# Loading a weight matrix in pairs of pieces to all partitions, with a re-ordered opening, in a retention and feed-forward kernel

## The chip, the cores and the metric

The kernel runs on one NeuronCore of a Trainium2 chip. TensorE (PE) multiplies matrices and writes PSUM; VectorE (DVE), ScalarE (ACT) and GpSimd (POOL) do element-wise work; SyncE (SP) issues most transfers between DRAM and SBUF, which the core's 16 DMA engines carry out. The engines run their own instruction streams in order and wait for one another through semaphores. The metric is the device time of one execution in microseconds (us), the median of several runs; less is better.

## The reference

q, k and v are [8 batches, 8 heads, 576 positions, 64] in float32. Each head is a retention layer: scores are q k^T / 8, multiplied by a decay gamma^(s - t) where s >= t and by 0 elsewhere, with gamma = 1 - 2^(-5 - head), and then multiplied by v. The result is laid out as x, [4608 tokens, 512 channels], channel = head x 64 + d. Then a feed-forward network: h = max(x w_in, 0), out = (h * h) w_out, with w_in [512, 2048] and w_out [2048, 512]. The two weights come as float64, as numpy makes them; the output is float32.

```python
scores = scale * np.matmul(q, k.transpose(0, 1, 3, 2))
ret = scores * Dmat[None, :, :, :]
attn_out = np.matmul(ret, v)
x = attn_out.transpose(0, 2, 1, 3).reshape(B * S, H * D)
h = np.maximum(x @ w_in, 0.0)
out = h * h @ w_out
```

## The kernel before

**Chunks.** The retention part goes over 40 chunks of up to 128 positions (five to a batch: four of 128, one of 64). For a chunk `load(i)` issues three transfers, for q, k and v, each as [positions, heads, 64]; `scale_q` and `scale_v` multiply q and v by powers of gamma (mostly on GpSimd); `turn(i)` transposes q and k on TensorE (L430) into a PSUM tile `t_ps` of two banks, and ScalarE (L434) and VectorE (L435) copy one bank each into the SBUF tile `qk`; `scores(i)` makes q k^T per half chunk of 64 positions (L461), and VectorE masks it (L471, from chunk 4 on L473). `retain_a`, `retain_b` and `retain_c` multiply with v (L559), add the contribution of the running state (L508) and let the state grow (L553); ScalarE copies the state (L487) and the finished piece of x (L536) to SBUF. From chunk 11 on a chunk is turned in another way (`flip`, L404 and L419).

**Weights.** w_in is used as 16 pieces of [512, 128], `pieces[0..15]`. A piece is fetched by `fetch_w` (L206) as raw 64-bit words into one of six places, and turned into float32 by `round_parts`: `one` (L220) takes the exponents, `two` (L224) the upper fraction bits, `beside` (L228, L229, ScalarE) makes the scale and the lower fraction, `three`, `four` and `five` (L232, L235, L238) put the number together. `convert(n)` issues the next n of these parts; `N_ALONE` says from which piece on the first two parts of a piece are put ahead of the last three of the one before. In SBUF a piece has partition p = 64 b + d, b = 0 or 1, d = 0..63, and column block c = 0..3, for row 256 b + 64 c + d of w_in. Before the change one piece is two transfers, one for each b, to 64 partitions each.

**The feed-forward part.** Tokens go in 9 blocks of 512. For block 0 `first_in(j)` multiplies all or half of its x with piece j (L664: four matmuls, 512 or 256 columns), takes max(.., 0) (L669) and squares it (L672). From block 1 on the products follow a Strassen-like scheme of seven products for eight (`ffn_in`, L700; the groups h_a, h_b, h_c), and the second matrix product (L1042) follows after all chunks are done. Squared values go to DRAM (`g_dram`) and come back for the second product.

**What sets the order.** The order of every engine's instructions is written out in the program: the calls from L845 to L901 for chunks 0 to 4, then a loop over the chunks (L902) in which `ffn(i, half)` interleaves feed-forward steps, with a table of points (`PACE`) for how many. Engines take their instructions in exactly that order, also SP its transfers, so a transfer that must wait for a buffer holds all behind it. For the first block the loop does three `step`s per chunk, a `convert(6)` beside each (L791 to L796); the second halves of the pieces whose first half was done in the opening (`N_HALF` = 3) are steps too. `fetch_raw(n)` fetches the next n pieces if a place is free; after the opening each finished piece calls it.

**Unread products.** `warm` (L824) issues matmuls on a constant tile whose result nobody reads. There are two forms: 128x128 on the whole array, and pairs on quarters of it, 64 rows by 512 columns.

Of the kernel before, what the change touches and what calls it, by code (L numbers as in the profile page):

```python
# [9 lines left out]
F32 = mybir.dt.float32  # L10
# [30 lines left out]
def kernel(  # L41
# [62 lines left out]
    work3 = first.enter_context(tc.tile_pool(name="work3", bufs=3))  # L104
    work2 = first.enter_context(tc.tile_pool(name="work2", bufs=2))
    ps_x = first.enter_context(tc.tile_pool(name="ps_x", bufs=1, space=PS))
    ps_t = first.enter_context(tc.tile_pool(name="ps_t", bufs=1, space=PS))
    ps_u = first.enter_context(tc.tile_pool(name="ps_u", bufs=1, space=PS))

# [20 lines left out]
    def load(i, names="qkv"):  # L132
# [4 lines left out]
        for name, pool, src in (("q", ld3, q), ("k", ld5, k), ("v", ld4, v)):  # L137
            if name not in names:
# [7 lines left out]

    pieces = [(0, m, e) for m in range(N_M) for e in range(2)]
    pieces += [(1, mq + mh * N_MQ, e) for mq in range(N_MQ) for mh in range(2) for e in range(2)]  # L150
    N_W1 = N_DF
    N_ALONE = 4
    N_HALF = 3
    stage = [W[5].rearrange("p (o s f) -> p o s f", o=4, s=NP),
             W[6][:, 0:3 * NP * 128].rearrange("p (o s f) -> p o s f", o=3, s=NP)]
    N_RAW = 6
    raw_all = [W[4 + j // 3][:, (j % 3) * 1024:(j % 3 + 1) * 1024] for j in range(N_RAW)]
    exp_all = [W[4 + j][:, 3072:3584] for j in range(3)]
    wide = moe_w_in.dtype != F32

    def raw_of(j):
        return raw_all[j % N_RAW] if j < N_W1 else raw_all[(j - N_W1) % 3]

    def exp_of(j):
        return exp_all[j % 2] if j < N_W1 else exp_all[2 * (j % 2)]

    def rows(half, n=64):
        return slice(64 * half, 64 * half + n)

    def piece_src(j):  # L170
        wi, m, e = pieces[j]
        f = (m + e * N_M) * 128
        return moe_w_out[f:f + 128, :].rearrange("p (c f) -> p c f", c=N_DM)

    def in_parts(j):

        wi, m, e = pieces[j]
        f = (m + e * N_M) * 128  # L180
        for half in range(2):
            of = slice(half * d_model // 2, (half + 1) * d_model // 2)
            yield rows(half), moe_w_in[of, f:f + 128].rearrange("(c p) f -> p c f", p=D)

    def piece_dst(j):
        wi, m, e = pieces[j]
# [5 lines left out]
    def as_dst(j, t):  # L192

        if pieces[j][0] == 0:
            return t.rearrange("p (c f) -> p c f", c=N_DM)
        return t.rearrange("p (o s f) -> p o s f", o=2, s=2)

    def fetch_w(j):
        if j >= len(pieces) or not wide:
            return  # L200
        to = raw_of(j).bitcast(I64)
        if pieces[j][0]:
            nc.sync.dma_start(to.rearrange("p (c f) -> p c f", c=N_DM), piece_src(j))
        else:
            for at, part in in_parts(j):
                nc.sync.dma_start(to[at].rearrange("p (c f) -> p c f", c=N_DM), part)  # L206

    def round_parts(j):
        words = raw_of(j).bitcast(U32).rearrange("p (n two) -> p n two", two=2)
        lo, hi = words[:, :, 0], words[:, :, 1]
        frac = raw_of(j).rearrange("p (n two) -> p n two", two=2)[:, :, 0]
        exp = exp_of(j).bitcast(U32)
        t = piece_dst(j)
        bits = t.bitcast(U32)

        def one():
            nc.vector.tensor_scalar(exp, hi, 20, 0x7FF, op0=ALU.logical_shift_right, op1=ALU.bitwise_and)  # L220

        def two():

            nc.vector.tensor_scalar(bits, as_dst(j, hi), 0xFFFFF, 0x100000, op0=ALU.bitwise_and, op1=ALU.bitwise_or)  # L224

        def beside():

            nc.scalar.activation(exp, exp, AF.Relu, bias=exp_bias[:, 0:1], scale=2.0 ** 23)  # L228
            nc.scalar.activation(frac, lo, AF.Copy, scale=2.0 ** -52)  # L229

        def three():
            nc.vector.scalar_tensor_tensor(t, bits, 2.0 ** -20, as_dst(j, frac), op0=ALU.mult, op1=ALU.add)  # L232

        def four():
            nc.vector.tensor_tensor(t, t, as_dst(j, exp_of(j)), op=ALU.mult)  # L235

        def five():
            nc.vector.scalar_tensor_tensor(bits, as_dst(j, hi), 0x80000000, bits, op0=ALU.bitwise_and, op1=ALU.bitwise_or)  # L238

        if not wide:  # L240
            if pieces[j][0]:
                return [lambda: nc.sync.dma_start(t.rearrange("p o s f -> p (o s) f"), piece_src(j))] + [lambda: None] * 5
            return [lambda: [nc.sync.dma_start(t[at], part)
                             for at, part in in_parts(j)]] + [lambda: None] * 5
        return [one, two, beside, three, four, five]

    def sum_w_in(mp):
# [51 lines left out]
    def fetch_raw(count):  # L299

        for _ in range(count):
            if n_raw[0] < min(N_W1, n_made[0] + N_RAW):
                fetch_w(n_raw[0])
                n_raw[0] += 1


    def w_in_parts():
# [34 lines left out]
    fetch_raw(1)  # L342
    load(1, "v")
    load(2)
    fetch_raw(2)

    make_identity(nc, ident)

# [31 lines left out]
    def scale_q(i, engine):  # L380
        ci, cs = chunks[i][1], chunks[i][3]
        t = loaded[i][0][:cs]
        engine.tensor_tensor(t, t, dv[:cs, :, NCH + ci:NCH + ci + 1].to_broadcast([cs, H, D]), op=ALU.mult)  # L383
# [2 lines left out]


    N_TURN = 11
    N_ONE = N_TURN - 1
    moves = []  # L390

    def new_qk(i):
        t = work3.tile([128, 2, HP, C], F32, tag="qk", name="qk")
        st[i]["qT"], st[i]["kT"] = t[:, 0, :, :], t[:, 1, :, :]
        return t
# [23 lines left out]
            nc.scalar.copy(*moves.pop(0)[2:])  # L419
            count -= 1  # L420

    def turn(i):

        cs = chunks[i][3]
        n_h = cs // CH
        p = ps_t.tile([128, 2, 512], F32, tag="t", name="t_ps").rearrange("p h (j d t) -> p h j d t", j=2, d=HP)
        for j in (1, 0):
            for hp in range(HP):
                for h in range(n_h):
                    nc.tensor.transpose(p[:, h, j, hp, :], loaded[i][j][rows(h), 2 * hp:2 * hp + 2, :],  # L430
                                        ident[rows(h), rows(h)])
        to = new_qk(i)[:, :, :, :cs].rearrange("p j d (h t) -> p j d h t", h=n_h)
        if n_h == 2:
            nc.scalar.copy(to[:, :, :, 0, :], p[:, 0, :, :, :])  # L434
            nc.vector.tensor_copy(to[:, :, :, 1, :], p[:, 1, :, :, :])  # L435
        else:
            nc.scalar.copy(to[:, 1].rearrange("p d h t -> p h d t"), p[:, :n_h, 1, :, :])
            nc.vector.tensor_copy(to[:, 0].rearrange("p d h t -> p h d t"), p[:, :n_h, 0, :, :])

    def scores(i, part=False):  # L440

        b_, ci, c0, cs = chunks[i]
        if i < N_EARLY:

            sc = [ps_f.tile([128, 512], F32, tag="f", name="sc_ps")[:, 0:256].rearrange("p (h t) -> p h t", h=HP) for e in range(2)]
        else:
            both = ps_t.tile([128, 2, 512], F32, tag="t", name="sc_ps")[:, :, 0:256].rearrange("p e (h t) -> p e h t", h=HP)
            sc = [both[:, e, :, :] for e in range(2)]
        st[i]["sc"] = sc
        st[i]["both"] = None if i < N_EARLY else both  # L450
        if part:
            return
        for hp in range(HP):
            score(i, hp)
        masked(i)
# [365 lines left out]
        held[0] = busy[0] = False  # L821


    def warm(count, wide):  # L824
        t = ps_f.tile([128, 512], F32, tag="f", name="idle_ps")
        for _ in range(count):
            if wide:
                nc.tensor.matmul(t[:, 0:128], lhsT=idle, rhs=idle, start=True, stop=True)
            else:
                for b in range(2):  # L830
                    nc.tensor.matmul(t[rows(b), :], lhsT=idle[rows(0), rows(b)], rhs=idle[rows(0), 0:1].to_broadcast([64, 512]),
                                     start=True, stop=True, skip_group_check=True)

    def loads(i):
        if i < N_TURN - 1:
# [6 lines left out]
        if i + 3 < N_CH:  # L842
            load(i + 3, "v")

    warm(6, True)  # L845
    scale_q(0, nc.vector)
    turn(0)
    load(3)
    scores(0)
    scale_q(1, nc.gpsimd)  # L850
    warm(1, False)
    turn(1)
    fetch_raw(1)
    retain_a(0)
    convert(3)
    scores(1)
    scale_q(2, nc.gpsimd)
    retain_b(0)
# [1 line left out]
    load(4)  # L860
    fetch_raw(2)
    convert(2)
    retain_a(1)
    turn(2)
    convert(1)
    retain_b(1)
    retain_c(1)
    load(5)
    fetch_raw(1)
    convert(3)  # L870
    first_in(0, (0,))
    convert(1)
    scores(2)
    scale_q(3, nc.gpsimd)
    retain_a(2)
    convert(2)
    turn(3)
    first_in(1, (0,))
    convert(3)
    retain_b(2)  # L880
    retain_c(2)
    load(6)
    fetch_raw(1)
    convert(1)
    scores(3)
    convert(2)
    scale_q(4, nc.gpsimd)
    first_in(2, (0,))
    convert(3)
    retain_a(3)  # L890
    turn(4)
    retain_b(3)
    retain_c(3)
    load(7)
    fetch_raw(2)
    step()
    scores(4)
    convert(3)
    scale_q(5, nc.gpsimd)
    step()  # L900
    convert(5)  # L901
    for i in range(N_EARLY + 1, N_CH + 1):  # L902
        if i > N_ONE:
            move(C, i)
# [287 lines left out]
```

## Time and profile before

| | |
|---|---|
| three runs | 967.30, 967.76, 970.39 us; median 967.76 |
| the profiled execution | 970.93 us, its span on the core 969.2 us |
| granted TensorE clock, mean | 0.989 |
| TensorE busy | 949.6 us, 98% of the span |
| VectorE busy | 783.1 us, 81% |
| ScalarE busy | 337.3 us, 35% |
| GpSimd busy | 133.3 us, 14% |
| chain that ended last | TensorE 92%, VectorE 4%, transfers 2% |
| first products of block 0 (L664), in all | 61.7 us, 152 rows |

The profile comes from one execution. A row of a group gives the source line, the engine, the operation, the tile written and the tiles read, the shape, the count, and the busy time with the mean of one. A window row gives for a stretch the busy time and count of each engine, then the granted TensorE clock (1.00 is full), the mean busy share of the 16 DMA engines (packets can overlap, so it can pass 1) and what they moved. A wait row gives who waited, for whom, how long in total, how often, and the longest. The chain of waits follows the work that ended last back to the start, step by step. The slices cut the span into 40 equal parts of 24.2 us; a digit is a tenth of busy share.

### The profile page before, as it was taken

The page shows a single profiled execution, that of the slowest core. Times are in us where ns is not written, and L with a number is a line of the kernel's source. Part 1 is how long each engine was busy: PE and PEld are TensorE (multiplying, and loading weights), DVE is VectorE, ACT ScalarE, POOL GpSimd, SP SyncE. Part 2 cuts the span into 40 slices and gives each one's busy share as a digit, 9 for nine tenths or more (in the row PEclk, how much of TensorE's full clock was granted, in tenths as well). Part 3 has the DMA queues.
Part 4 walks back from the last instruction along what each step waited for, and adds up shares of the span by engine and source line. Part 5 has one row for each costly group of instructions (what it writes and reads, how often), then busy time and mean ns, then how long its engine had stood idle before and what let it go on. Part 6 is the DMA issues. An engine that isn't in the chain of part 4 may idle for free.

```text
span 969.2 us, 23541 instructions
## 1 busy us (share of the span) xinstructions
PE 949.6 (98%) x10000; PEld 852.4 (88%) x10000; DVE 783.1 (81%) x1447; ACT 337.3 (35%) x808; POOL 133.3 (14%) x121
## 2 busy tenths in 40 slices
PE   7799999999999999999999999999999999999998
PEld 6645688888888888888888899999999999999998
DVE  3599799988889887987976597887888787787876
ACT  3345375765765767657621000000000000000000
POOL 2221233123133123122110000000000000000000
PEclk7999999999999999999999999999999999999999
DMA  9996667676857867776168966445354454524251
GB/s 197 202 226 165 153 167 211 179 226 208 208 151 220 242 166 203 199 213 170 61 253 330 366 238 244 165 158 185 115 202 155 159 195 170 203 99 174 88 175 44
DMA packets 169705, 181.39 MB, mean 187 GB/s; under 512 B 115840, under 2 KB 130176, under 8 KB 162944
## 3 DMA queue, kind: packets, MB, share of 16 engines
q1 hardware_dynamic: 167520, 179.37, 61.7%
q8 instruction: 78, 1.28, 0.6%
q10 hardware_dynamic: 2080, 0.52, 0.3%
q14 instruction: 27, 0.22, 0.1%
HBM read 109.36 MB, written 70.52 MB: 186 GB/s over the span
## 4 chain that ended last, share of the span: by engine, by line
PE 92%; DVE 4%; DMA 2%; issue 1%; ACT 1%; SPq 0%; DVEq 0%
PE o_b L1042 17%; PE h_b L700 16%; PE o_a L1042 11%; PE o_c L1042 11%; PE h_a L700 11%; PE h_c L700 10%; PE h_ps L664 6%; PE x_ps L559 3%; PE sc_ps L461 2%; PE u_ps L553 1%; DMA g<-g_dram 1%; PE x_ps L596 1%; PE t_ps L430 1%; PE x_ps L508 1%; DMA q_ld<-in_q_dram 0%
## 5 line engine op out<-in xcount | busy, mean ns | idle before, releaser
L700 PE MATMUL h_b<-room,w 128*128 128x256 f32 x768 | 183.6, 382 | 2.8 <-DVE room L719 1.8
L419 ACT COPY qk<-flip 32x256 f32<-32x256 f32 x416 | 167.3, 402 | 6.2
L700 PEld LDWEIGHTS h_b<-room,w 128*128 128x128 f32 x768 | 144.3, 190 | 24.3 <-DVE room L719 2.6
L1042 PE MATMUL o_b<-w,room 128*128 128x128 f32 x1168 | 144.4, 275 | 0.2 <-DVE room L994 0.2
L1042 PEld LDWEIGHTS o_b<-w,room 128*128 128x128 f32 x1168 | 137.2, 192 | 0.4 <-DVE room L994 0.4
L1042 PE MATMUL o_c<-w,room 128*128 128x128 f32 x1008 | 123.0, 275 | 0.0
L700 PE MATMUL h_a<-room,w 128*128 128x256 f32 x512 | 122.0, 381 | 0.0
L700 PE MATMUL h_c<-room,w 128*128 128x256 f32 x512 | 121.7, 380 | 0.0
L1042 PEld LDWEIGHTS o_c<-w,room 128*128 128x128 f32 x1008 | 117.7, 192 | 0.0
L1056 ACT COPY r<-o_a 128x128 f32<-128x128 f32 x53 | 14.2, 267 | 272.8 <-PE o_a L1042 236.9
L700 PEld LDWEIGHTS h_a<-room,w 128*128 128x128 f32 x512 | 96.5, 190 | 13.8 <-issue 0.5
L700 PEld LDWEIGHTS h_c<-room,w 128*128 128x128 f32 x512 | 96.7, 190 | 13.3
L1042 PE MATMUL o_a<-w,a 128*128 128x128 f32 x688 | 85.7, 275 | 0.0
L717 POOL TENSOR_TENSOR room<-room 128x512 f32<-128x512 f32 x32 | 36.1, 1129 | 337.5 <-ACT room L716 326.2
L1042 PEld LDWEIGHTS o_a<-w,a 128*128 128x128 f32 x688 | 81.2, 192 | 0.1
L707 DVE SCALAR_TENSOR_TENSOR room<-room 128x512 f32<-128x512 f32 x96 | 70.0, 730 | 3.3
L664 PE MATMUL h_ps<-room,w 128*128 128x512 f32 (+1 forms) x152 | 61.7, 555 | 3.6 <-DVE w L238 2.3
L559 PEld LDWEIGHTS x_ps<-qk,v_ld 64*64 64x64 f32 x1152 | 45.7, 140 | 15.7 <-issue 13.8
L559 PE MATMUL x_ps<-qk,v_ld 64*64 64x64 f32 x1152 | 56.7, 229 | 1.7 <-DVE qk L471 1.0
L383 POOL TENSOR_TENSOR q_ld<-q_ld,dv 128x512 f32<-128x512 f32 (+1 forms) x39 | 45.6, 1170 | 78.9 <-DMA q_ld<-in_q_dram 72.6
L480 POOL TENSOR_TENSOR v_ld<-v_ld,dv 128x512 f32<-128x512 f32 (+1 forms) x40 | 52.7, 1318 | 16.9 <-DMA v_ld<-in_v_dram 16.9
L664 PEld LDWEIGHTS h_ps<-room,w 128*128 128x128 f32 x152 | 28.7, 197 | 27.7 <-issue 23.6
(107 smaller groups left out, 1350.9 us busy)
## 6 DMA issues: line engine op xcount, KB each, us to landing
g_dram<-room SPq DMA_DIRECT2D x32, 1280.0 KB, 5.7
a<-g_dram SPq DMA_DIRECT2D x30, 1024.0 KB, 5.8
room<-g_dram SPq DMA_DIRECT2D x15, 1024.0 KB, 6.1
w<-w_dram SPq DMA_DIRECT2D x7, 1792.0 KB, 9.9
out_dram<-room SPq DMA_DIRECT2D x17, 512.0 KB, 3.3
q_ld<-in_q_dram SPq DMA_DIRECT2D x32, 256.0 KB, 6.3
w<-in_moe_w_in_dram SPq DMA_DIRECT2D x32, 256.0 KB, 5.8
w<-in_moe_w_out_dram SPq DMA_DIRECT2D x16, 512.0 KB, 4.2
```

Source lines behind the costliest of these rows:

```text
L383: engine.tensor_tensor(t, t, dv[:cs, :, NCH + ci:NCH + ci + 1].to_broadcast([cs, H, D]), op=ALU.mult)
L419: nc.scalar.copy(*moves.pop(0)[2:])
L430: nc.tensor.transpose(p[:, h, j, hp, :], loaded[i][j][rows(h), 2 * hp:2 * hp + 2, :], ident[rows(h), rows(h)])
L461: nc.tensor.matmul(st[i]["sc"][e][rows(h), hp, :], lhsT=st[i]["kT"][rows(e), hp, t], rhs=st[i]["qT"][rows(e), hp, t], start=True, stop=Tru ...
L480: nc.gpsimd.tensor_tensor(vs[:cs], vs[:cs], dv[:cs, :, ci:ci + 1].to_broadcast([cs, H, D]), op=ALU.mult)
L559: return [lambda hp=hp, e=e, b=b: nc.tensor.matmul(x_at(hp, e, b, h), lhsT=s["vs"][rows(h), 2 * hp + e, :], rhs=s["ret"][rows(h), e, hp, : ...
L664: nc.tensor.matmul(p.rearrange("p h t -> p (h t)"), lhsT=w[:, c, :], rhs=xT[0][:, c, lo * HT:hi * HT], start=(c == 0), stop=(c == N_DM - 1))
L700: nc.tensor.matmul(p[:, mm, :], lhsT=w[:, c, :], rhs=xs[n][right][:, c, :], start=(j in OPENS and mm == 0 and c == 0), stop=(j in CLOSES a ...
L707: nc.vector.scalar_tensor_tensor(t, t, 0.0, t, op0=ALU.max, op1=ALU.mult)
L717: nc.gpsimd.tensor_tensor(g["A11"], g["A11"], g["A11"], op=ALU.mult)
L1042: nc.tensor.matmul(p, lhsT=s["lefts"][left][:, m, :], rhs=w_out[j][:, m, WO_SLOT[right], :], start=(i in OPENS and m == 0), stop=(i in CLO ...
L1056: nc.scalar.copy(r[:, 0, 0:128], p)
```

## The change

The change has four parts. (1) w_in is fetched by `fetch_in` to all 128 partitions in four transfers, one for each column block c: pieces 0 and 1 alone, the others two pieces at a time, 256 columns together, into one of three places for pairs. The order of the pieces changes so that two neighbours in w_in's columns follow one another. The parts of `round_parts` read the raw words through patterns with one more dimension. (2) Chunks 0 to 3 are turned into two PSUM tiles of one bank each (`ps_e`) instead of one tile of two; `turn` is split in `turn_in` and `turn_out`, and chunk 2 has both of its copies on ScalarE. The pool is closed before chunk 4, and the one tile of two banks takes its place. (3) The unread products have one form, 128 rows by 256 columns on the whole array; there are 14 of them in seven places. (4) The calls of the opening stand in another order, with one half product less (`N_HALF` = 2) and one whole product more before the loop.

```diff
-    pieces = [(0, m, e) for m in range(N_M) for e in range(2)]
+    pieces = [(0, 2 * mp + mm, e) for mp in range(N_MP) for e in range(2) for mm in range(2)]
-    N_HALF = 3
+    N_HALF = 2
-    N_RAW = 6
-    raw_all = [W[4 + j // 3][:, (j % 3) * 1024:(j % 3 + 1) * 1024] for j in range(N_RAW)]
+    N_PAIR = 3
+    raw_one = [W[4 + j][:, 2048:3072] for j in range(2)]
+    raw_two = [W[4 + j][:, 0:2048] for j in range(N_PAIR)]
...
-    def in_parts(j):
-        wi, m, e = pieces[j]
-        f = (m + e * N_M) * 128
-        for half in range(2):
-            of = slice(half * d_model // 2, (half + 1) * d_model // 2)
-            yield rows(half), moe_w_in[of, f:f + 128].rearrange("(c p) f -> p c f", p=D)
+    def in_rows(c, j, count):
+        wi, m, e = pieces[j]
+        f = (m + e * N_M) * 128
+        return moe_w_in.rearrange("(b c d) f -> c b d f", b=2, d=D)[c][:, :, f:f + 128 * count]
...
-            for at, part in in_parts(j):
-                nc.sync.dma_start(to[at].rearrange("p (c f) -> p c f", c=N_DM), part)
+    def fetch_in(j, count):
+        to = (raw_one[j] if count == 1 else raw_two[(j // 2 - 1) % N_PAIR]).bitcast(I64).rearrange("p (c f) -> p c f", c=N_DM)
+        for c in range(N_DM):
+            nc.sync.dma_start(to[:, c, :], in_rows(c, j, count))
...
     def fetch_raw(count):
         for _ in range(count):
-            if n_raw[0] < min(N_W1, n_made[0] + N_RAW):
-                fetch_w(n_raw[0])
-                n_raw[0] += 1
+            j = n_raw[0]
+            if j < N_W1 and (j < 2 * N_PAIR + 2 or n_made[0] >= j - 2 * N_PAIR + 2):
+                count = 1 if j < 2 else 2
+                fetch_in(j, count)
+                n_raw[0] += count
...
-    def turn(i):
-        p = ps_t.tile([128, 2, 512], F32, tag="t", name="t_ps").rearrange("p h (j d t) -> p h j d t", j=2, d=HP)
+    def turn_in(i, js=(1, 0)):
+            if i < N_EARLY:
+                p = [ps_e.tile([128, 512], F32, tag=f"e{h}", name="t_ps") for h in range(2)]
+            else:
+                t = ps_t[0].tile([128, 2, 512], F32, tag="t", name="t_ps")
+                p = [t[:, h, :] for h in range(2)]
...
+    def turn_out(i, engines=(0, 1)):
+        copies = (nc.scalar.copy, nc.vector.tensor_copy)
+            for h in range(2):
+                copies[engines[h]](to[:, :, :, CH * h:CH * h + CH], p[h])
...
-    def warm(count, wide):
+    def warm(count):
+            nc.tensor.matmul(t[:, 0:256], lhsT=idle, rhs=idle[:, 0:1].to_broadcast([128, 256]), start=True, stop=True)
```

The opening, as it stands after the change:

```python
    warm(5)
    scale_q(0, nc.vector)
    turn_in(0, (1,))
    scale_q(1, nc.gpsimd)
    warm(3)
    turn_in(0, (0,))
    turn_out(0)
    load(3)
    warm(1)
    scores(0)
    turn(1)
    fetch_raw(1)
    retain_a(0)
    scores(1)
    scale_q(2, nc.gpsimd)
    retain_b(0)
    retain_c(0)
    load(4)
    fetch_raw(2)
    convert(2)
    warm(1)
    retain_a(1)
    convert(1)
    warm(1)
    retain_b(1)
    retain_c(1)
    load(5)
    convert(3)
    turn(2, (0, 0))
    warm(2)
    scores(2)
    scale_q(3, nc.gpsimd)
    convert(2)
    first_in(0, (0,))
    retain_a(2)
    convert(1)
    retain_b(2)
    retain_c(2)
    load(6)
    convert(3)
    first_in(1, (0,))
    turn(3)
    warm(1)
    scores(3)
    scale_q(4, nc.gpsimd)
    convert(3)
    retain_a(3)
    early.close()
    ps_t[0] = first.enter_context(tc.tile_pool(name="ps_t", bufs=1, space=PS))
    turn(4)
    convert(3)
    retain_b(3)
    retain_c(3)
    load(7)
    fetch_raw(1)
    step()
    step()
    scores(4)
    convert(6)
    scale_q(5, nc.gpsimd)
    step()
    convert(6)
```

## The prediction

> **What bounds the kernel now.** I read the page's slices first, then the ten-microsecond windows, then the chain of waits, then the transfers.
>
> ```profile
> PE   7799999999999999999999999999999999999998
> ...
> DVE  3599799988889887987976597887888787787876
> ...
> PEclk7999999999999999999999999999999999999999
> DMA  9996667676857867776168966445354454524251
> ```
>
> One slice is 24.2 us. TensorE is busy in all but the first two or three slices, so from about 50 us on whatever shifts TensorE's stream shifts the end one for one. The transfer engines are full in exactly the first three slices. The windows show the same opening (busy us of PE, PEld, DVE, ACT, POOL, then granted clock, transfer share, GB/s):
>
> ```profile
> 0.00:10.00 10.00, 5.64 (x62) 4.74 (x64) 1.65 (x4) 1.87 (x2) 3.42 (x12) 0.88 0.97 182
> 10.00:20.00 10.00, 9.14 (x202) 7.00 (x202) 5.04 (x9) 3.97 (x8) 3.18 (x3) 0.50 1.17 219
> ...
> 30.00:40.00 10.00, 6.63 (x147) 5.13 (x141) 4.52 (x10) 3.40 (x8) 2.86 (x3) 0.83 1.11 205
> ...
> 50.00:60.00 10.00, 9.53 (x64) 4.55 (x64) 9.83 (x17) 3.31 (x7) 3.04 (x2) 0.83 0.97 190
> ```
>
> and so do narrower windows, and the first 60 us in one:
>
> ```profile
> 53.00:58.00 5.00, 5.00 (x10) 2.14 (x9) 4.93 (x10) 1.01 (x2) 0.39 (x1) 0.76 1.08 224
> 63.50:65.00 1.50, 1.50 (x5) 0.47 (x3) 1.45 (x3) 0.64 (x2) 0.00 (x0) 1.00 1.05 346
> ...
> 0.00:60.00 60.00, 47.09 (x744) 34.26 (x744) 33.08 (x61) 20.76 (x41) 17.27 (x24) 0.83 1.07 198
> ```
>
> In the first 60 us TensorE idles 60 - 47.1 = 12.9 us and runs part of the rest at half clock (0.50 from 10 to 20 us). The last chain pieces of the first stage fix my mark, the end of the first block's last product:
>
> ```profile
> 107.15 3.63 PE h_ps L664 x8
> 110.78 1.73 PE h_a L700 x8
> ```
>
> The mark is 110.78 us. The same work stands ahead of it in both kernels, and from there the streams are alike: time after = time before + shift of the mark. The profiled execution took 970.93 us (span 969.2 us); the median of the three runs is 967.76 us, 3.2 us less, and I put the shift on the median.
>
> The waits that the change touches (engine, line, releaser: us in total, times, longest), and the transfers of w_in (32 of 256 KB, us from issue to landing):
>
> ```profile
> DVE qk L435 <- ACT qk L434: 9.3, 7, 2.6
> ...
> PE h_ps L664 <- DVE w L238: 2.3, 1, 2.3
> ```
> ```profile
> w<-in_moe_w_in_dram SPq DMA_DIRECT2D x32, 256.0 KB, 5.8
> ```
>
> **The change part by part.**
>
> *The w_in transfers.* Before: 32 transfers, each 64 partitions by 4 rows of 1 KB; the source's outermost step counts 64. After: pieces 0 and 1 are four transfers each of 128 KB (1 KB rows), the other 14 go in seven pairs of four transfers of 256 KB (2 KB rows): 8 + 28 = 36. Four more issues at 0.62 us (the median issue of this line) are 2.5 us on SP, which is in no chain piece of the opening. Pieces 4 to 7 now stand in SP's queue ahead of the loads of chunks 5 to 7; the loads of chunks 8 and 9 stand behind pairs (10,11) and (14,15). What matters is the new source pattern: "b=2" outermost, then 64 rows, because the two partition halves come from two places in w_in. Every transfer of q, k, v, w_in, w_out, g and out in the trace has an outermost count of 64 or 128. No row shows one of 2, nor how a transfer is dealt to the 16 engines. I bound it from both sides.
>
> Best: dealt to all 16, and 2 KB rows move at the 346 GB/s of the window 63.5 to 65 us (stores of 2 KB rows) instead of the 224 GB/s of 53 to 58 us (nearly pure w_in): the seven pairs, 7.34 MB, need 21 us instead of 33 us, in a stretch where the transfers are full.
>
> Worst: dealt by the outermost count, hence to two engines. An engine moved 224 / 16 = 14.0 GB/s with 1 KB rows and 346 / 16 = 21.6 GB/s with 2 KB rows; the page's fastest slice is 366 GB/s, 22.9 each. The two engines then carry, in queue order: start 2 us; their sixteenth of the loads of chunks 0 to 8, 8.5 x 786 KB / 16 = 0.42 MB at 198 / 16 = 12.4 GB/s, 34 us; pieces 0 and 1, 1.05 MB, at 28 to 46 GB/s for the two, 37 to 23 us, middle 30; the pairs at 45.8 GB/s, 160 us; their sixteenth of 2 MB of g stores, 6 us. Sum 232 us until the last pair lands (at 14 GB/s an engine the pairs alone take 262 us). Then VectorE and ScalarE convert it (two steps of 0.42, ScalarE's 0.71 + 0.67, three of 0.69: 4.3 us), TensorE does its two products (3.63 us each, up to twice that where the clock has dropped, say 9 us) with one chunk's turn of some 2 us between: 15 us. The mark moves from 110.8 to 247 us, by 136 us. Everything that covered a transfer before is gone: TensorE's order is written out, and it waits at each first-block product for its piece. What is late next is chunks 3 to 9, whose q, k and v land only when their share on those two engines has come through.
>
> I take the two engines, because the outermost count is the only property in which the new transfers differ from all that the trace shows to run at full rate, and a transfer cut along it gives two shares. The nearest rows by size (1 KB and 2 KB rows) price it; both ends stay for the range.
>
> On this the Trainium skill speaks twice. "DMA: Bandwidth & Descriptors", section "Why a DMA increments its semaphore by 16 and not by 1", says that the number of engines is the largest, up to 16, that divides the slowest count of both patterns, which would be 2 here. Its section "Rules for kernel authors" advises one transfer to 128 partitions over two to halves, which alone would favour the change. By the first the time would be the 1104 us worked out below, by the second the 960 us of rival A; no row here decides.
>
> *Two PSUM tiles for turned chunks.* VectorE's copy no longer waits for ScalarE's (0.59 us) for chunks 0, 1 and 3: -1.9 us on the chain. Chunk 2 has both on ScalarE, 1.2 us against 1.3: nothing.
>
> *Unread products.* Away: six of 128x128 (2.93 us, in a wait) and the half-array pair, which stands on the chain with 1.8 us. Added: 14 of 128x256, at most 2 x 2.93 / 6 = 0.98 us each while slow and 0.49 when fast. Eight lie in the 4.6 us of idle before chunk 0's turn; of the other six about half, 1.5 us, are on the chain. In return the half-clock stretch from 8 to 22 us (12.3 us busy at 0.53) could run at full clock: at most 6 us, half of it on the chain, -3.
>
> *Order.* Piece 2's half product goes (2.3 us wait, and 1.0 us because its 3.0 us were slow against 2.0 for its like): -3.3 us; its work returns in a whole product, and one half product more is done before the loop. On POOL chunk 1's q goes ahead of chunk 0's v: v is 1.06 us later, used only after scores(0), hidden; if that cover is gone, +1. The conversions keep their instructions, 0.42 and 0.69 us; the extra dimension of their patterns I put at 0, at worst some 0.1 us on each of 16 x 5, of which VectorE's slack (45.4 busy of 50 us from 60 to 110 us) covers half.
>
> Sum of all but the transfers: -1.9 - 1.8 - 3 - 3.3 + 1.5 = -8.5 us. In the two-engine case none of it survives, since the mark waits for the last pair. So: 967.8 + 136 = 1104 us.
>
> **The rivals.**
>
> A, *all 16 engines take the new transfers*, chance 0.31. For it: the opening's transfers at 219 GB/s and share above 1 are the thing to relieve, and the destination is 128 partitions. Then -8.5 us and perhaps 1 us more from earlier pieces, less that VectorE at 9.83 of 10 us in 50 to 60 us leaves little room to convert faster: 960 us. Ends: all 12.9 us of idle and about 9 us of half clock gained, 946 us; nothing, 968 us.
>
> B, *transfers spread, but the new order stalls*, chance 0.06: the two conversions put before chunk 5's turn copies hold those up on VectorE and ScalarE (TensorE waits 2.03 us for that copy already, in front of its scores at 50.47 us). Each piece ahead of it is 2.9 us on VectorE; from three pieces on, 8.7 us, it eats the 8.5 us gain. 972 us, 968 to 980.
>
> C, *no effect*, chance 0.03: prologue gains are given back in 50 to 110 us, where VectorE is busy 45 us of 50. 967 us.
>
> **How the numbers follow.** Two engines has 0.60, at 1104 us; its own range is 1061 us (at 26.6 GB/s an engine, a sixteenth of the 426 GB/s of the fastest stretches between 505 and 540 us, the pairs need 138 us instead of 160; with pieces 0 and 1 at 23 instead of 30 and the loads at 20 instead of 34 the sum falls by 43 us) to 1190 us (towards 1221 us, all w_in at 14 GB/s an engine). A has 0.31, more than 2 in 10, so the range must reach it: 954 us (a tenth of A lies below) to 1180 us (an eighth of the likeliest case lies above), leaving out about 0.11. Within 0.3%, some 3 us, a measurement of this kernel can't tell from no change. Faster 0.31 from A, same 0.03 from C, slower 0.60 + 0.06.
>
> **What would show it.** Two engines: landing of the w_in transfers at tens of us instead of 5.8; transfer share in the first slices far below 1, GB/s near 50; TensorE waiting for VectorE's L249 (the conversion's last step) and for q and k loads until about 230 us, half clock in between; the mark near 247 us. All sixteen: landing near 6 us, the mark near 102 us, the clock near 1.0 from 10 us on, no wait of VectorE's copy on ScalarE's for chunks 0 to 3. B: the mark at 111 us or later with TensorE waiting for chunk 5's copies. The prediction fails if the outermost count doesn't set the dealing, or if an engine alone is much faster or slower than a sixteenth of the full rate.

## The result, and the profile after

The changed kernel takes 1096.3 us (median of four runs, 1092.15 to 1096.44); the kernel before, run beside it, 968.52 us. The ratio is 1.1307, 95% interval 1.1274 to 1.134: slower by 127.8 us. The profiled execution took 1096.2 us, its span 1094.5 us, at a mean granted clock of 0.939.

The slices of the changed kernel (one is 27.4 us):

```profile
PE   6441645589999999999999999999999999999998
...
DVE  2221343369997989888978865888877877888776
PEclk8765866799999999999999999999999999999999
DMA  5213322457768757866862499754545355245341
```

TensorE is full from the tenth slice on, before it was from the third. In the slices ahead of that everything is low at once: TensorE, VectorE, the clock, and the transfers, which were full in the first three slices before. A core on which nobody works is waiting for something that none of these rows counts as busy. Windows of the same stretch show what (busy us of PE, PEld, DVE, ACT, POOL, then granted clock, transfer share, GB/s):

```profile
60.00:80.00 20.00, 13.14 (x112) 9.16 (x112) 7.48 (x15) 5.42 (x11) 2.10 (x2) 0.76 0.14 49
80.00:100.00 20.00, 0.00 (x0) 0.00 (x0) 2.13 (x5) 1.28 (x2) 0.00 (x0) 0.50 0.18 62
...
63.00:89.00 26.00, 11.81 (x104) 7.92 (x96) 9.07 (x18) 5.01 (x10) 0.38 (x1) 0.70 0.13 52
```

In the last window almost nothing but w_in moves. The share of 0.13 is 2 of 16 engines (0.125), and the rate stays at some 51 GB/s (49 to 53 in four such stretches), which is 25.5 GB/s for each of the two. SyncE's queue shows the same from the side of the issue (start, duration, count):

```profile
56.30 33.46 SPq L215 DMA_DIRECT2D w<-in_moe_w_in_dram  x8
89.87 4.94 SPq L144 DMA_DIRECT2D q_ld<-in_q_dram  x1
```

The eight transfers of two pairs take 33.46 us to issue, 4.2 us each, where the median issue of this line before took 0.62 us, and the next chunk's q is issued only behind them. The waits of the first 260 us (total, times, longest):

```profile
POOL q_ld L395 <- DMA q_ld<-in_q_dram: 205.6, 11, 45.4
DVE w L231 <- DMA w<-in_moe_w_in_dram: 93.1, 8, 16.6
...
PE t_ps L449 <- DMA k_ld<-in_k_dram: 43.6, 2, 30.4
PE h_ps L693 <- DVE w L249: 38.9, 5, 15.2
```

Before, VectorE's conversions waited for no piece of w_in that these rows would show, and the h products waited 2.3 us for VectorE. Now the conversions wait for the pairs, the products for the conversions, and the turns of chunks for k. The end of the first block, on TensorE:

```profile
225.73 5.40 PE L693 MATMUL h_ps<-room,w 128*128 128x512 f32 x8 [2.98 <-DVE w L249]
232.60 1.99 PE L729 MATMUL h_a<-room,w 128*128 128x256 f32 x8
```

I take the start of the first h_a product as the mark from here on. It was at 110.62 us and is at 232.60 us: a shift of 122.0 us, against 125.3 us in the span. The loss is made ahead of the mark.

### The profile page after: what moved, and what is told of

It is laid out like the page before. It is cut to its first block, busy times and chain, and to the rows that moved or that the text cites. A ratio compares the mean times of both kernels' runs of the same rounds, so it can differ in the third digit from the quotient of the medians.

```text
span 1094.5 us, 23549 instructions
## 1 busy us (share of the span) xinstructions
PE 970.5 (89%) x10004; PEld 861.4 (79%) x10004; DVE 782.6 (72%) x1445; ACT 338.1 (31%) x808; POOL 134.2 (12%) x121
## 5 line engine op out<-in xcount | busy, mean ns | idle before, releaser
L729 PE MATMUL h_c<-room,w 128*128 128x256 f32 x512 | 122.0, 381 | 0.0
L693 PE MATMUL h_ps<-room,w 128*128 128x512 f32 (+1 forms) x144 | 74.8, 679 | 39.6 <-DVE w L249 38.9
L693 PEld LDWEIGHTS h_ps<-room,w 128*128 128x128 f32 x144 | 33.3, 242 | 72.6 <-issue 35.8
L231 DVE TENSOR_SCALAR w<-w 128x512 uint32<-128x512 uint32 x32 | 16.0, 501 | 93.1 <-DMA w<-in_moe_w_in_dram 93.1
```

The costliest lines, as they stand in the source:

```text
L693: nc.tensor.matmul(p.rearrange("p h t -> p (h t)"), lhsT=w[:, c, :], rhs=xT[0][:, c, lo * HT:hi * HT], start=(c == 0), stop=(c == N_DM - 1))
L729: nc.tensor.matmul(p[:, mm, :], lhsT=w[:, c, :], rhs=xs[n][right][:, c, :], start=(j in OPENS and mm == 0 and c == 0), stop=(j in CLOSES a ...
```

## The experiments

Each time is a median, with its ratio to the kernel before that ran beside it on the same chip, and the 95% interval.

### The dealing

**One part undone: halves of 64 rows.** The changed kernel with its pairs, its order and its PSUM tiles, but each fetch in two transfers as before:

```diff
-        for c in range(N_DM):
-            nc.sync.dma_start(to[:, c, :], in_rows(c, j, count))
+        f = (pieces[j][1] + pieces[j][2] * N_M) * 128
+        for b in range(2):
+            of = slice(b * d_model // 2, (b + 1) * d_model // 2)
+            nc.sync.dma_start(to[rows(b)], moe_w_in[of, f:f + 128 * count].rearrange("(c p) f -> p c f", p=D))
```

> The changed kernel with one thing undone: each fetch of w_in goes out as two transfers, one to each half of the partitions, with 64 rows outermost in the source, instead of four to all partitions with 2 outermost. Rows stay 2 KB for the pairs, order, tiles and unread products stay as changed. Theory (a transfer is dealt to the engines by the outermost count, 2 here): the loss is gone and the rest of the change shows, 960 us (952 to 968), no stretch at 51 GB/s. Rival (the loss is in the pairs, the 2 KB rows or the new order): near 1096 us still.

Measured: 980.37 us, ratio 1.0127 (1.011 to 1.0143), mark at 120.65 us. 116 of the 127.8 us are gone with the four transfers of the new pattern. The rest of the change doesn't gain, though: it loses 12 us, so the time misses the theory's range as well.

**That part alone.** The kernel before, with a piece fetched in four transfers of the new pattern and nothing else changed:

```diff
-            for at, part in in_parts(j):
-                nc.sync.dma_start(to[at].rearrange("p (c f) -> p c f", c=N_DM), part)
+            wi, m, e = pieces[j]
+            f = (m + e * N_M) * 128
+            for c in range(N_DM):
+                nc.sync.dma_start(to.rearrange("p (c f) -> p c f", c=N_DM)[:, c, :],
+                                  moe_w_in.rearrange("(b c d) f -> c b d f", b=2, d=D)[c][:, :, f:f + 128])
```

> The kernel before with one thing changed: each piece of w_in goes out as four transfers of 128 KB to all partitions with 2 outermost in the source; pieces still one at a time, 1 KB rows, old order. Theory (two engines): 8.39 MB at 51 GB/s or a little less for the shorter rows need 164 to 190 us, and with their sixteenth of the loads of chunks and a tail of 15 us the first block ends at 215 to 245 us instead of 111: 1070 to 1105 us. Rival (the pairs, 2 KB rows or the new order are at fault): 968 us.

Measured: 1088.73 us, ratio 1.1243 (1.1224 to 1.1262), mark at 231.20 us, both inside the theory's ranges. The pattern alone makes the loss, in single pieces of 1 KB rows too.

**The same 36 transfers, another outermost count.** Only the source of the changed kernel's transfers differs:

```diff
-        return moe_w_in.rearrange("(b c d) f -> c b d f", b=2, d=D)[c][:, :, f:f + 128 * count]
+        return moe_w_in.rearrange("(c p) f -> c p f", p=128)[c][:, f:f + 128 * count]
```

> The changed kernel with the same 36 transfers, the same bytes, row lengths, partitions and order, but each reads 128 neighbouring rows of w_in, so that the outermost count of the source is 128 instead of 2. The rows of w_in then meet the wrong rows of x: the first matrix product is of a w_in with permuted rows, all else is as it was. Theory (outermost count): 958 us (950 to 966), w_in alone at over 224 GB/s. Rival (128 partitions or the shape of the transfers are at fault): near 1096 us.

Measured: 976.44 us, ratio 1.0082 (1.0066 to 1.0098), mark at 112.88 us. Number, size and destination of the transfers are those of the changed kernel, so neither their count nor the write to 128 partitions can be the cause. The time is above the 950 to 966 us of the theory, because the rest of the change loses here too.

**Four and eight.** The same line with `b=4` and `b=8`.

> The changed kernel's 36 transfers with 4 outermost in the source instead of 2; the rows of w_in come in another order, so the product is not the reference's, while the amount of data and of arithmetic is the same. Theory (a transfer is dealt over as many engines as its outermost count, at the 25.5 GB/s an engine that the changed kernel showed at 63-89 us): w_in moves at about 102 GB/s, 4 MB take some 41 us of the four engines plus the q, k and v that stand in them; the first h_a product starts at 120-140 us instead of 113 (128 outermost) or 233 (2 outermost), time 985-1010 us. Rival (two outermost is a special case, anything above is dealt to all): 974-979 us as with 128.

> As with four, but 8 outermost (the rows of w_in in another order again, so the product is not the reference's). Theory: about 204 GB/s, which is more than the 40 us a pair-by-pair need of 4 MB in some 80 us; first h_a product at 112-118 us, time 974-983 us. If the loss goes on in proportion to the share of idle engines (rival: any count below 16 costs in the same proportion): 2 to 128 outermost cost 120 us for 14 of 16 engines idle, 8 of 16 idle would cost 40-70 us and the time be 1015-1045 us.

Both texts give the amount wrongly: w_in is 8.4 MB (16 pieces of 512 KB), not 4. At 102 GB/s that is 82 us, not 41. Measured with four: 1017.2 us, ratio 1.0503 (1.0487 to 1.0519), mark at 153.85 us. With eight: 977.44 us, ratio 1.011 (1.0064 to 1.0155), mark at 120.48 us. Windows in which little but w_in moves, the first of the kernel with four, the second with eight:

```profile
45.00:55.00 10.00, 9.33 (x67) 6.83 (x60) 3.74 (x8) 1.79 (x5) 0.00 (x0) 0.63 0.27 103
```
```profile
34.00:36.00 2.00, 1.42 (x44) 1.25 (x48) 1.47 (x2) 1.70 (x4) 1.08 (x1) 0.92 0.52 202
```

The shares are 4 and 8 of 16 (0.25 and 0.50), and 103 and 202 GB/s make 25.8 and 25.3 GB/s an engine. A transfer of these two kernels reads other rows of w_in than one with 2 or 128 outermost, and the rate follows the count, so it isn't which rows are read. Two, four, eight and 128 outermost put the mark at 232.6, 153.9, 120.5 and 112.9 us. The profiled execution with eight is a long one, 981.57 us, where two others took 973 us; by the ratios eight can't be told from 128 rows. The time behaves as a queue does: with eight engines w_in needs some 41 us and is covered as well as with 128 rows, as far as the time shows; with four it needs 82 us and no longer fits beside the other loads on the same four, with two it needs 164 us and sets the end. The forecast of 985 to 1010 us for four was too low, at least in part because of the wrong amount. "Only two is special" would have been 974 to 979 us for four, and falls.

**The last three pairs alone.** The kernel with halves, with the two-outermost form for pieces 10 to 15 only:

```diff
+        if j >= 10:
+            for c in range(N_DM):
+                nc.sync.dma_start(to[:, c, :], in_rows(c, j, count))
+            return
```

> As the run with halves, but the last three pairs (pieces 10 to 15) keep the four transfers with 2 outermost. Theory (two engines at 25.5 GB/s each, queued one after another): 3 x 1.05 MB at 51 GB/s are 62 us, and with the chunk loads and stores between them some 72 us, from about 50 us on; last landing near 122 us, the first block's end near 138 us instead of 101: 985 to 1010 us. Rival (what costs is the delay of the first chunks' loads in the opening, not the rate): 960 us.

Measured: 1020.74 us, ratio 1.0541 (1.0525 to 1.0557), mark at 158.33 us. Against the kernel with halves the mark goes from 120.65 by 37.7 us. The shift is what the text has; it was added to a base that I had put at 960 us and that is 980, so the time lies 11 us above the range. The loss goes with the amount of w_in that goes through the two engines: 12 us a MB for these 3.15 MB, 13 us a MB (112 us) for all 8.39 MB.

### What is left of the change

The forecast had the rest of the change at -8.5 us. It measures +8 us with 128 rows and +12 us with halves.

**Pairs alone.** The kernel before with pairs in halves. The order of the opening, the PSUM tile, the unread products and `N_HALF` are the old ones; the pieces, their places, the patterns of the conversions and `fetch_raw` are those of the pairs.

```diff
-    pieces = [(0, m, e) for m in range(N_M) for e in range(2)]
+    pieces = [(0, 2 * mp + mm, e) for mp in range(N_MP) for e in range(2) for mm in range(2)]
...
-            for at, part in in_parts(j):
-                nc.sync.dma_start(to[at].rearrange("p (c f) -> p c f", c=N_DM), part)
...
+        for b in range(2):
+            of = slice(b * d_model // 2, (b + 1) * d_model // 2)
+            nc.sync.dma_start(to[rows(b)], moe_w_in[of, f:f + 128 * count].rearrange("(c p) f -> p c f", p=D))
```

> The kernel before with one part of the change alone, without the two-outermost source: w_in fetched two pieces at a time (rows of 2 KB, halves of 64 rows), with the old order of the opening, the one PSUM tile and the old unread products. Theory (the remaining loss sits in the new opening's order, which hands out one product more against the same conversions): 965-970 us, as before. Rival 1 (the pairs cost it, since a piece waits for its neighbour and a pair's buffer comes free only after both): 973-982 us. Rival 2 (half the transfers, rows twice as long, give w_in earlier): 955-963 us.

Measured: 976.92 us, ratio 1.0092 (1.0078 to 1.0107). The time is that of rival 1: pairs in halves lose 9 us by themselves. Its reason, a piece that waits for its neighbour, is not what the rows show: VectorE's conversions wait 1.8 us in all for w_in. On GpSimd in the kernel before, then in this one:

```profile
37.25 1.06 POOL L383 TENSOR_TENSOR q_ld<-q_ld,dv 128x512 f32<-128x512 f32 x1 [4.54 <-PE h_ps L664]
```
```profile
42.48 1.06 POOL L396 TENSOR_TENSOR q_ld<-q_ld,dv 128x512 f32<-128x512 f32 x1 [9.52 <-DMA q_ld<-in_q_dram]
```

Two pairs, 2.1 MB, stand in SyncE's queue right ahead of the loads of chunk 5, where two pieces, 1.05 MB, stood before. Its q was scaled at 37.25 us in the kernel before, after a wait for TensorE and not for the transfer; now it comes at 42.48 us, after a wait for the transfer. TensorE is busy 12.9 of the 20 us from 40 to 60 us, where it was 17.3. That this delay makes the 9 us is argued from these rows; no run moves the pairs elsewhere in the queue.

**128 rows without pairs.** The kernel before, a piece in one transfer of 128 neighbouring rows:

```diff
-            for at, part in in_parts(j):
-                nc.sync.dma_start(to[at].rearrange("p (c f) -> p c f", c=N_DM), part)
+            wi, m, e = pieces[j]
+            f = (m + e * N_M) * 128
+            nc.sync.dma_start(to.rearrange("p (c f) -> p c f", c=N_DM),
+                              moe_w_in[:, f:f + 128].rearrange("(c p) f -> p c f", p=128))
```

> The kernel before with one thing changed: a piece of w_in comes in one transfer of 128 neighbouring rows to all partitions instead of two of 64 rows (the rows of w_in then come in another order, so the product is not the reference's; amount of data and arithmetic as before). It keeps single pieces, the old opening, one PSUM tile and the old unread products. In the runs with pairs, 128 rows took 4 us less than halves (976.4 against 980.4). Theory A (the 10 us or so that remain of the loss belong to the pairs, which put 512 KB in front of the q, k and v of the opening): without pairs 128 rows give 962-967 us. Theory B (the width of the transfer is worth nothing while single pieces are fetched in time): 967-969 us.

Measured: 969.88 us, ratio 1.0006 (0.9995 to 1.0017). By the ratio this is theory B: the kernel before doesn't gain from it.

**128 rows, the new opening, no pairs.** The same fetch in the changed kernel, with the pieces in the old order and places and the calls of `fetch_raw` spread to suit single pieces.

```diff
-    pieces = [(0, 2 * mp + mm, e) for mp in range(N_MP) for e in range(2) for mm in range(2)]
+    pieces = [(0, m, e) for m in range(N_M) for e in range(2)]
...
-        for c in range(N_DM):
-            nc.sync.dma_start(to[:, c, :], in_rows(c, j, count))
...
+            nc.sync.dma_start(to.rearrange("p (c f) -> p c f", c=N_DM),
+                              moe_w_in[:, f:f + 128].rearrange("(c p) f -> p c f", p=128))
```

> The run before this one in the list (single pieces, each in one transfer of 128 neighbouring rows; product not the reference's) plus the rest of the change: the new order of the opening, the turned chunks in two PSUM tiles, the wide unread products and one product less handed out by halves. What is left out of the change is only the pairs. Theory A (the loss that remains is the pairs' alone): 955-966 us, not slower than the same without the new opening; the forecast's gain of some 8 us may show. Theory C (the new opening loses by itself, since it gives one product more for the same conversions): 970-977 us, as with pairs of 128 rows (976.4).

("One product less handed out by halves" is `N_HALF` = 2; the three product steps before the loop are all there.) Measured: 976.83 us, ratio 1.0077 (1.0054 to 1.0101), the same as with pairs (976.44), and inside theory C's range; theory A falls. So with 128 rows the pairs cost nothing and the new opening, its tiles and unread products cost 7 us; with halves the pairs cost 9 us and the opening some 3 more. The two losses don't add up.

**One product step less before the loop.** From the opening of the changed kernel, first with halves, then with 128 rows:

```diff
     scale_q(5, nc.gpsimd)
-    step()
     convert(6)
```

> The changed kernel with halves of 64 rows, and with the last of the three product steps before the block loop taken out, so that the opening hands out one whole product less and the conversion of the parts is that much further ahead when the loop begins. Theory (what is left of the loss, 12 us with halves and 8 us with 128 rows outermost, comes from conversions that run closer ahead of the products: TensorE waits for VectorE's last part of a piece in 70-110 us): 960-970 us, and the waits of h products on VectorE before the first block's end fall below 3 us. Rival (it comes from the loads, which are larger and start in another order, or from the order of the opening itself): 977-984 us, no change against 980.4.

> The changed kernel with 128 neighbouring rows outermost (pairs, new opening, two PSUM tiles, wide unread products; the rows of w_in in another order, so the product is not the reference's), and the last of the three product steps before the block loop taken out. With the step in place it took 976.4 us (1.0082 of before), and its h products waited 7.9 us on VectorE's last conversion part. Theory (the new opening gives one product more against the same conversions, and that is what it loses): the waits of h products on VectorE go below 3 us and the time is 966-971 us, level with before. Rival (the order of the opening, the PSUM tiles or the unread products lose by something else): 974-978 us. With halves the same edit went from 980.4 to 976.0 us.

Measured: 976.04 us, ratio 1.0089 (1.007 to 1.0108), instead of 980.37; and 972.59 us, ratio 1.0042 (1.0028 to 1.0055), instead of 976.44. Both go down by about 4 us (3.7 and 3.9 by the ratios). The halves run misses the theory's range and lies below the rival's; the 128-row run lies between the two. The waits of the h products fall from 7.9 to 2.6 us with halves, as the theory says, and to 3.4 us with 128 rows. The waits for the conversion, first in the 128-row kernel with the step, then without it:

```profile
DVE w L243 <- ACT w L240: 12.3, 10, 3.1
...
PE h_ps L693 <- DVE w L249: 7.9, 5, 2.6
```
```profile
PE h_ps L693 <- DVE w L249: 3.4, 2, 3.0
```

So 4.5 us of waits go and 4 us of time. In the kernel before, then with the new opening and the step in place, TensorE had this in the loop:

```profile
100.00:110.00 10.00, 10.00 (x137) 5.48 (x136) 7.54 (x11) 2.59 (x6) 3.59 (x3) 1.00 0.33 75
```
```profile
100.00:110.00 10.00, 7.42 (x53) 3.42 (x52) 7.19 (x8) 1.58 (x4) 4.38 (x3) 0.87 0.27 62
```

Without the step it is busy for all 10 us again. The 4 us in time are shown by both runs, and they are half of what the new opening loses with 128 rows. That they are these waits is argued from the rows: the two profiled executions took 973.93 us with the step and 974.14 us without it, so they don't show the 4 us themselves. The other 4 us stay open. In the profiled execution of the run without the step the mark stands at 111.14 us, 0.5 us behind that of before; the other 2.7 us of its span come after an idle near 424 us that has no releaser (last section). I have no experiment that separates the PSUM tiles, the unread products and the order of calls.

**A layout that makes the 128 rows usable.** In the kernels with 128 neighbouring rows the partitions don't match those of x. This one deals the heads otherwise, so that they match, in the kernel before with single pieces of 128 rows:

```diff
-    HEADS = [(hp, e, hp // (HP // 2)) for hp in range(HP) for e in range(2)]
+    HEADS = [(hp, e, hp % 2) for hp in range(HP) for e in range(2)]
...
-                    nc.tensor.transpose(p[:, h, j, hp, :], loaded[i][j][rows(h), 2 * hp:2 * hp + 2, :],
-                                        ident[rows(h), rows(h)])
+                    for e in range(2):
+                        nc.tensor.matmul(p[rows(e), h, j, hp, :], lhsT=loaded[i][j][rows(h), HP * e + hp, :],
+                                            rhs=ident[rows(h), rows(h)], start=True, stop=True, skip_group_check=True)
...
```

> The first kernel of this list with the heads dealt to the partitions in another order (heads hp and hp+4 share a turned tile, even heads stand in partitions 0 to 63 of x and odd ones in 64 to 127), so that 128 neighbouring rows of w_in are what the product needs. It costs a turn by 64x64 quarters with plain products in the first 11 chunks and two half transposes instead of one on VectorE after them. If these are hidden: the time of the first kernel of this list, 962-968 us. If the quarters cost TensorE time: 970-978 us.

Measured: 973.48 us, ratio 1.0055 (1.0037 to 1.0072), the mark at 114.56 us: in the second range of the text, 3.6 us more than with the heads as they were. That the quarters cost it is not shown, since VectorE's two half transposes came with them. No version here beats the kernel before.

## Why the prediction was right, and where it was not

**Two engines.** Right in the step that carried it, that the outermost count sets how many engines take a transfer: two, four and eight gave 2, 4 and 8 sixteenths of the share. The prediction set two rules of the Trainium skill against each other; they are not opposed. "DMA: Bandwidth & Descriptors", "Why a DMA increments its semaphore by 16 and not by 1", agrees with all four counts run here. Its "Rules for kernel authors" prefers one transfer to 128 partitions over two halves, on the ground that both halves already run on all 16 engines, and the same table says that an outermost count below 16 confines a transfer to at most that many engines; so both sections give two here. With a count of two the halves win by 116 us, and with 128 rows the single transfer is worth nothing measurable in the time (ratio 1.0006).

**The price of an engine.** The term that was off is "the pairs at 45.8 GB/s, 160 us". I took 22.9 GB/s an engine from a stretch in which all 16 worked. Two engines alone make 51 GB/s, which gives 7.34 MB / 51 = 144 us, 16 us less. The other end in the text, 26.6 GB/s, was nearer. The second sign of failing in the text, an engine alone much faster than a sixteenth of the full rate, was in part met: 25.5 GB/s against the 14.0 of the stretch of w_in alone. The 21.6 GB/s that the text gives for 2 KB rows came from a mixed stretch, in which 154 of 336 packets were under 2 KB. The last pair's conversion starts at 206.8 us instead of 232; I can't split the other 9 us among the start, the loads and the first two pieces.

**The tail.** Put at 15 us after the last pair, it took 25.8 us (206.8 to 232.6). I had put two products at 9 us there. There were three, 9.31 us for two in a row and 5.40 us for the last, at a granted clock of 0.66 from 200 to 220 us, with chunk work between them:

```profile
206.82 0.43 DVE L231 TENSOR_SCALAR w<-w 128x512 uint32<-128x512 uint32 x1 [16.59 <-DMA w<-in_moe_w_in_dram]
```
```profile
212.18 9.31 PE L693 MATMUL h_ps<-room,w 128*128 128x512 f32 x16 [1.35 <-DVE w L249]
```

So +11 against -25: the mark came at 232.6 us instead of 247, and its shift is 122 us instead of 136. That the time is off by 8 us and not by 14 is luck: the span moved 3.3 us more than the mark, and the medians moved 2.5 us more than the span (127.8 against 125.3). The upper end of 1221 us adds up to some 1213 us from the terms that the text gives, and the transfer row has a 9 in slice 23 too, not only in the first three; neither changes the forecast.

**From the mark on all alike.** Nearly: in the changed kernel the span moved 3.3 us more than the mark. 1.0 us of that is an idle without releaser, 2.02 us at 547 us instead of 1.00 us at 424 us. Another 1.7 us is the clock behind it: the two groups of eight products that follow start 3.13 and 2.01 us before the next, where such a group takes 1.73 us at full clock. 0.6 us stay open.

**The other four parts at -8.5 us.** Wrong in sign, which the time doesn't show because the pairs cover it. Two of the gains that I listed can be seen: the clock from 10 to 20 us is 1.00 in the 128-row kernel, not 0.50, and the 9.3 us in which VectorE's copies of whole chunks waited for ScalarE's in the first 150 us have no row any more (1.5 us are left for the half chunk, 5.5 before). But the clock can't be put down to the new unread products. The kernel before with pairs, which has the old ones, also has 1.00 in this stretch, while with the new ones halves had 0.83:

```profile
10.00:20.00 10.00, 8.71 (x244) 6.74 (x240) 5.55 (x11) 4.47 (x9) 3.20 (x3) 1.00 1.27 211
```

The gains are not worth what I put on them. The step that failed is the one on the order, "its work returns in a whole product, and one half product more is done before the loop", taken as a gain of 3.3 us without asking what it does to the look-ahead of the conversions. Taking a product out of the opening gives 4 us back. I put the larger fetches' effect on the q, k and v behind them at nothing, though I had seen them in the queue: pairs in halves cost 9 us.

**The rivals.** A, all 16 engines, would have been 976 to 980 us and not 960: had the dealing been as in A, the forecast for it would have had the wrong sign. B named a place, chunk 5's copies. No row shows it late while the step is in place; without it the scores there wait 4.11 us with halves and 2.19 us with 128 rows, against 2.03 us before. B's time, 972 us with 968 to 980, was about what a good dealing gives, for another reason. C, "given back in 50 to 110 us, where VectorE is busy", had the place and, by the rows, the mechanism, but more is given back than was gained.

**The signs to look for.** Share, the wait for L249 and the low clock were as written; the rate was near 50 GB/s where w_in moved alone, and 53 to 120 in the first nine slices. The landing times were not to be read: the transfers of w_in have none in the changed kernel's rows, and the duration of their issue shows the delay instead.

## What to carry to other kernels

Before a transfer is reshaped, look at the outermost count of its source and its destination: a count of two for a partition tile that comes from two places takes 14 of 16 engines away, and the loads that stand behind it in the queue wait with it. Price such a transfer by amount / (engines x rate of one engine), 25 to 26 GB/s here, and see whether it still fits beside what hides it; eight engines could not be told from all 16 in the time, four lost 5%. Here an opening that hands out products earlier did not gain, and by the rows what feeds them had not moved up as well.

## What the runs showed of the hardware that I had not expected

**An engine alone is faster than a sixteenth.** It made 25.3 to 25.8 GB/s with two, four or eight at work on rows of 2 KB, while all 16 in the nearly pure w_in stretch of the kernel before made 224 / 16 = 14.0 on rows of 1 KB. The length of the rows is not the reason: in the kernel before with the two-outermost pattern, two engines alone moved rows of 1 KB at 48 GB/s (120 to 125 us, share 0.14), 24 for each.

**128 rows in one transfer move more than two halves.** From 20 to 40 us, with the transfer engines full, the kernel with halves of 2 KB rows moved no more than before with 1 KB rows (206 and 198 GB/s); with 128 rows outermost and 2 KB it was 256, and with 128 rows and 1 KB rows 224 (210 with the new opening). The kernel with halves, then the changed one with 128 rows:

```profile
20.00:40.00 20.00, 14.03 (x297) 10.77 (x301) 9.78 (x19) 6.59 (x14) 4.22 (x4) 0.83 1.08 206
```
```profile
20.00:40.00 20.00, 15.07 (x282) 12.07 (x280) 9.69 (x19) 6.82 (x15) 5.90 (x6) 0.91 1.04 256
```

I don't know why. A half also goes to 64 partitions and the others go to 128, no run separates the two, and the mix of loads in the window is not quite the same.

**An idle that belongs to nobody, and the clock behind it.** Near 424 us TensorE pauses without a releaser, for 1.00 us in the profiled execution of before, 2.10 us in that of the 128-row kernel with one step less, and 0.49 us in that of before with 128 rows. Before, then the 128-row kernel with one step less:

```profile
423.63 1.35 PE L700 MATMUL h_b<-room,w 128*128 128x256 f32 x5 [1.00 <-issue]
424.82 1.89 PE L700 MATMUL h_c<-room,w 128*128 128x256 f32 x8
```
```profile
424.18 0.59 PE L729 MATMUL h_a<-room,w 128*128 128x256 f32 x2 [2.10 <-issue]
424.61 3.46 PE L729 MATMUL h_b<-room,w 128*128 128x256 f32 x8
```

After the pause of 2.10 us the granted clock is 0.50 (426 to 428 us) and eight products take 3.46 us instead of 1.89. The same follows the pause of 2.02 us in the changed kernel (0.50 from 549 to 551 us), while after 1.00 us before and 1.75 us in the 128-row kernel with single pieces and the new opening it stays at 1.00. Pause and clock together make the 2.7 us by which the kernel with one step less falls back behind its mark (1.1 and 1.7 us). So a pause costs more than its length here, and profiles of these kernels that differ by 2 or 3 us are told apart by their runs, not by their spans.
